# Sliding-window attention with a squared-ReLU MLP: a reordered issue plan, the last store on another queue, and the mask distances on another engine

## The chip, the cores and the metric

The kernel runs on one core of a Trainium2 chip. Five engines of that core work side by side: TensorE (PE in the profile: matrix products and transposes), VectorE (DVE), ScalarE (ACT), GpSimd (POOL) and SyncE (SP). Each takes its own instructions strictly in order, and semaphores hold an instruction back until what it needs is there. Transfers run on 16 DMA engines and are issued here from three queues: GpSimd's (loads that convert to bf16), SyncE's and ScalarE's. The metric is the device time of one execution in microseconds; lower is better. Four runs of the kernel before took between 317.31 and 318.31 us, median 317.45.

## The reference: what is computed

Attention over a window of 128 positions with a distance penalty, and a two-layer MLP on its output:

```python
# q, k, v: (8 batches, 8 heads, 576 positions, 64), float32
scores = scale * np.matmul(q, k.transpose(0, 1, 3, 2))       # scale = 1/8
rel = pos[:, None] - pos[None, :]
slopes = 2.0 ** (-8.0 * (np.arange(H) + 1) / H)
bias = slopes[:, None, None] * (-np.abs(rel))[None]
mask = (rel >= 0) & (rel < window)                             # window = 128
scores = np.where(mask, scores + bias[None], -1e9)
attn = np.exp(scores - np.max(scores, axis=-1, keepdims=True))
attn = attn / (np.sum(attn, axis=-1, keepdims=True) + 1e-09)
x = np.matmul(attn, v).transpose(0, 2, 1, 3).reshape(4608, 512)
h = x @ w_in                                                   # w_in: 512 x 2048
g = np.maximum(h, 0.0) ** 2
out = g @ w_out                                                # w_out: 2048 x 512
```

## The kernel before

**Blocks and jobs.** The 576 positions of a batch are four blocks of 128 and one of 64, 40 blocks in all. `seq` lists them in the order of work and numbers them `m` = 0 to 39: first the eight first blocks (0 to 7), then pair after pair of batches. A query block sees its own key block and the one before, so a job is a "diag" (one or two first blocks, `DIAG`), a "full" (own and previous block) or a "half" (the two 64-position blocks of a pair of batches). Attention output is collected in `xT`, transposed, in ranges of 128 columns (`ranges`); two half blocks share a range. In the kernel before, the last range is the pair of half blocks of batches 6 and 7.

**Steps of a job.** In brackets stands the name that the planner gives a step. GpSimd's queue loads K and Q (`lkq`, L387) and V (`lv`, L392). K and Q are transposed: for blocks below `N_PE` = 9 by TensorE (`tp`, L443, eight 128x128 transposes) with copies out of PSUM (`ev`); for the others by a DMA transpose from SyncE's queue (`kqT`, L429). Scores (`s`, L499), exponentials on ScalarE (`e`, L523), a multiplication by the mask on VectorE (`m`, L531 to L538), attention values (`pv`, L566: a row of ones in V gives the softmax sum), a reciprocal (`r`, L584) and a scaling (`n`, L588). The result is transposed into `xT`: below `N_PE` by TensorE (`xp`, L608) and a copy (`x`), whole or, below `N_CUT` = 4, in two parts; above it by a DMA transpose from SyncE (`x`, L596).

**The MLP.** It works in nine groups `g` of 512 tokens, four ranges each. The up-projection of group 0 is cut into pieces of 128 tokens and of groups 1 and 2 into pieces of 256 (`u`, L700); later groups take 512 at a time (`fc`, L716). A piece's result is in PSUM; ScalarE takes the ReLU into bf16 (`relu`, L671) and VectorE squares it (`sq`, L662). The down-projection `o` (L742) runs per range in four pieces of four matmuls, each needing one quarter of `w_out`; a finished range is copied out of PSUM by ScalarE or VectorE (`oe`, L271 or L273) and stored from SyncE's queue (`st`, L761). The very last range is cut into columns 0 to 383 and 384 to 511 (`CUT`), each with a copy and a store of its own. A range of two half blocks needs two stores per part.

**Buffers that tie steps together.** PSUM has eight banks: two tagged "h" (up-projection pieces, `tp`, `xp`, and the values of the first `N_PVH` = 1 jobs), two "o" (down-projection), four "a" (scores, other values). A step that takes a bank waits until the step two (or four) before it with that tag has been copied out. K and Q have a ring of four buffers in SBUF.

**What sets the order.** All steps are put as tasks into a planner (`Plan`). Each has a key, a modelled length on each engine that could do it, the tasks it depends on, and the buffers that it takes and frees. `Plan.order` lists the tasks one at a time: of each engine's candidates, those that could start within `NEAR` ns of the earliest one compete, and the lowest key wins. The instructions are then issued in exactly that order. The keys come from the order of the MLP pieces (`work_list`), with a job placed `LEAD` = 320 key units ahead of the first piece that needs it, and from `DUE` for the first jobs. The loads at the start follow `FIRST` ("b3" is block 3's K, Q and V; "i2" and "o2" are quarters of `w_in` and `w_out`). A matmul group of which the planner expects that it waits over 200 ns is preceded by padding matmuls on a constant tile (`fill`, L252), in number 0.7 of the gap.

**The start.** GpSimd makes an iota of distances (L287). VectorE derives from it the identity (L294) and, for the own-block half (`part` 1), the mask distances (L300 and L301), from which ScalarE makes the eight heads' masks (L310). The half for the previous block (`part` 0) follows later in the same way. Eight warm-up matmuls on a constant tile (L413) run on TensorE meanwhile. Block 0's K and Q come through the queues of SyncE and ScalarE, everything else through GpSimd's queue, whose loads wait each for the one eight places ahead to have landed.

Of the kernel before, what the change touches and what calls it, by code (L numbers as in the profile page):

```python
# [15 lines left out]
FIRST = ["b0", "b1", "b2", "i0", "i1", "o0", "i2", "o1", "b3", "i3", "o2", "o3", "b4", "b5", "b6", "b7"]  # L16
DIAG = [[0], [1], [2], [3], [4, 5], [6, 7]]
N_PE = 9
N_CUT = 4
N_PVH = 1  # L20
N_WARM = 8
FILL = 0.7
LEAD = 320
# [5 lines left out]
DUE = {**{m: 200.0 * m - 1e5 for m in range(40)}, **{7: -40.0}}  # L29

# [26 lines left out]
class Plan:  # L57
# [8 lines left out]
    NEAR = {"PE": 25, "ACT": 250, "DVE": 60}  # L66
# [17 lines left out]
    def order(self):  # L84
        used = {tag: [] for tag in self.bufs}
# [90 lines left out]
def kernel(  # L176
# [23 lines left out]
    for b in range(0, B, 2):  # L200
# [5 lines left out]
        ranges.append([(b, HALF), (b + 1, HALF)])  # L206
        seq += ranges[-1]
# [49 lines left out]
    def act(n):  # L257
        return n * 0.95 + 115.0
# [4 lines left out]
    def dve_p(n, rate=1):  # L263
        return n / rate / 0.96 + 185.0
# [33 lines left out]
    def build_dist(part):  # L298
        op, lim = ((ALU.is_ge, float(window)), (ALU.is_lt, 0.0))[part]
        nc.vector.tensor_scalar(far[:, part], dist[:, part], lim, 1.0e6, op0=op, op1=ALU.mult)  # L300
        nc.vector.tensor_tensor(dist[:, part], dist[:, part], far[:, part], op=ALU.add)  # L301

    t_dist, t_mask, last_mask = [None, None], [[], []], None
    for part in (1, 0):
        key = EARLY + 2 if part else -1e5 + 1100
        t_dist[part] = plan.add({"DVE": 430.0}, key, lambda part=part: build_dist(part), [t_ident], name="dist",
                                later=0.0 if part else 18000.0)
        for p in range(H):
# [3 lines left out]
            t_mask[part].append(plan.add({"ACT": act(128)}, key + 1 + p, build_mask, [t_dist[part]], name="mask"))  # L312

    def ones(ts):
        for t in ts:
            nc.vector.memset(t[:, :, D:D + 1], 1.0)
    t_ones = [plan.add({"DVE": 320.0}, EARLY + 3, lambda: ones(tiles["v0"][0:2]), name="ones"),
              plan.add({"DVE": 900.0}, -1e5 + 300, lambda: ones(tiles["v0"][2:]), name="ones", later=11000.0),
              plan.add({"DVE": 1200.0}, -1e5 + 900, lambda: ones(tiles["v"]), name="ones", later=20000.0)]
# [37 lines left out]
    def load_block(m, key):  # L357
# [35 lines left out]
        l_v = plan.add({"POOL": 890.0}, key + 0.2, fetch_v, [t_zero] if kb == HALF else [], [s_v[m]],  # L393
# [28 lines left out]
    def transpose_kq(m, due):  # L422
# [12 lines left out]
        for i in range(2):  # L435
# [14 lines left out]
            for c0, c1 in pieces:  # L450
                def evac(i=i, st=st, c0=c0, c1=c1, e=len(evs[i])):
# [4 lines left out]
                    else:  # L456
# [4 lines left out]
                                       [t_tp[i]] + evs[i], [], [st], name=f"ev{m}.{i}"))  # L461
# [191 lines left out]
    def relu_square(g, slot, last_mm, key, out_of, fused):  # L653
# [12 lines left out]
        else:  # L666
            srt = Slot("rt")

            def relu():
                srt.tile = work.tile([128, 512], BF16, tag="rt", bufs=3, name="rt")  # L670
                nc.scalar.activation(srt.tile, slot.tile, AF.Relu, bias=0.0, scale=1.0)  # L671
            tr = plan.add({"ACT": act(512)}, key, relu, [last_mm], [srt], [slot], name=f"relu{g}")
            ts = plan.add({"DVE": dve(512, 2)}, key, lambda: square(srt.tile), [tr] + g_sq[g][:1], [], [srt],
                          name=f"sq{g}")
# [128 lines left out]
```

The softmax here doesn't subtract the row's maximum and nothing guards it: scores larger than these inputs give would overflow.

## Time and profile before

| | |
|---|---|
| Median of four runs | 317.45 us |
| The profiled execution | 317.51 us |
| Its span in the profile | 315.7 us |
| TensorE busy | 305.3 us (97%), 2810 matmuls |
| VectorE and ScalarE busy | 172.8 and 173.4 us (55% each) |
| GpSimd busy | 105.6 us (33%), nearly all issue of loads |
| L742 on TensorE | 592 matmuls, 143.0 us |
| L716 and L700 on TensorE | 384 and 512 matmuls, 96.7 and 46.7 us |
| Loads and stores | 39.14 MB |

The table is read as follows. The profiled execution's own time is 1.8 us over its span: the span runs from the first to the last event that the profiler records. A busy time adds the stretches in which at least one instruction of the engine runs. Matmuls of TensorE overlap: one of 128x512 is recorded with 379 ns, but they start 216 ns apart, so the number of matmuls times their distance, not their length, tells what a change of their number is worth. A group of four such matmuls takes 0.86 us of TensorE, a piece of 16 with 128 columns 0.89, a 128x128 transpose 0.055. Names like L742 are lines of the kernel before; in the changed kernel the same code stands some 20 lines further down.

### The profile page before, as it was taken

The numbers are of one execution on the slowest core, as the hardware profiler recorded it, in microseconds if no ns is written. First come the engines' busy times: TensorE is split into PE (matmuls) and PEld (weight loads), VectorE is DVE, ScalarE is ACT, GpSimd is POOL, SyncE is SP. The second block draws the span as 40 slices with busy tenths as digits, with TensorE's granted clock in tenths as the row PEclk, the third lists the DMA queues.
The fourth block names the chain that finished last, engine by engine and source line by source line (L and its number), as shares of the span: only waits on it lengthen the run. The fifth ranks groups of instructions, "written<-read, shape, count | busy, mean of one in ns | idle before, by whom it ended". The sixth has DMA issues, their size and how long they took to land.

```text
span 315.7 us, 7140 instructions
## 1 busy us (share of the span) xinstructions
PE 305.3 (97%) x2810; PEld 175.2 (55%) x2810; DVE 172.8 (55%) x494; ACT 173.4 (55%) x340; POOL 105.6 (33%) x131
## 2 busy tenths in 40 slices
PE   6789999999999999999999999999999999999994
PEld 3677767667777655555555455545445444444442
DVE  3755567666767667676676666666663222222111
ACT  5565466668566635675655665557743444444300
POOL 8835598543623855206746007200000000000000
PEclk9999999999999999999999999999999999999999
DMA  9999999999999999949999939952211000011112
GB/s 128 189 205 190 170 195 176 153 176 143 198 160 141 169 175 174 154 91 144 168 189 166 140 95 134 199 109 70 50 52 50 35 34 33 35 33 44 57 69 66
DMA packets 164130, 39.14 MB, mean 124 GB/s; under 512 B 154752, under 2 KB 159616, under 8 KB 164096
## 3 DMA queue, kind: packets, MB, share of 16 engines
q0 software_dynamic: 114656, 18.10, 83.1%
q1 hardware_dynamic: 49152, 20.33, 33.2%
q8 instruction: 22, 0.36, 0.5%
q10 hardware_dynamic: 288, 0.26, 0.3%
q14 instruction: 12, 0.10, 0.1%
HBM read 36.70 MB, written 9.44 MB: 146 GB/s over the span
## 4 chain that ended last, share of the span: by engine, by line
PE 88%; DMA 8%; POOL 2%; issue 0%; DVE 0%; POOLq 0%
PE o L742 39%; PE h L716 27%; PE h L700 11%; PE pv L566 6%; PE s L499 5%; DMA w_out_sb<-in_moe_w_out_dram 5%; DMA w_in_sb<-in_moe_w_in_dram 3%; POOL kq L387 1%; POOL vf L392 1%; PE tp L443 1%; PE xp L608 0%; POOL w_in_sb L340 0%; POOL dist L287 0%; DVE osb L271 0%; POOLq L287 0%
## 5 line engine op out<-in xcount | busy, mean ns | idle before, releaser
L742 PE MATMUL o<-w_out_sb,g 128*128 128x512 bf16 (+2 forms) x592 | 143.0, 373 | 0.6 <-DMA w_out_sb<-in_moe_w_out_dram 0.6
L671 ACT ACTIVATE rt<-h 128x512 bf16<-128x512 f32 x144 | 85.8, 609 | 95.8 <-PE h L716 69.9
L662 DVE TENSOR_TENSOR g<-rt 128x512 bf16<-128x512 bf16 x144 | 60.1, 420 | 76.3 <-ACT rt L671 76.1
L716 PE MATMUL h<-xT,w_in_sb 128*128 128x512 bf16 x384 | 96.7, 379 | 0.0
L742 PEld LDWEIGHTS <-g 128*128 128x128 bf16 x592 | 54.0, 98 | 56.3 <-issue 0.8
L523 ACT ACTIVATE P<-s 128x512 bf16<-128x512 f32 (+1 forms) x136 | 67.0, 582 | 8.7 <-PE s L499 8.6
L716 PEld LDWEIGHTS <-w_in_sb 128*128 128x128 bf16 x384 | 35.2, 98 | 39.3
L531 DVE TENSOR_TENSOR P<-P,masks 128x512 bf16<-128x512 bf16 (+1 forms) x112 | 44.6, 405 | 15.0 <-ACT P L523 10.3
L700 PE MATMUL h<-xT,w_in_sb 128*128 128x128 bf16 (+1 forms) x512 | 46.7, 246 | 2.2 <-DMA w_in_sb<-in_moe_w_in_dram 2.2
L392 POOL DMA_DIRECT2D vt<-in_v_dram x32 | 27.0, 846 | 51.8 <-PE pv L566 48.9
L387 POOL DMA_DIRECT2D kq<-in_k_dram x39 | 33.3, 855 | 29.8 <-DMA kqT<-kq 23.5
L700 PEld LDWEIGHTS <-w_in_sb 128*128 128x128 bf16 x512 | 38.6, 98 | 6.3 <-DMA w_in_sb<-in_moe_w_in_dram 2.6
L387 POOL DMA_DIRECT2D kq<-in_q_dram x39 | 33.5, 859 | 7.2 <-PE tp L443 2.9
L588 DVE TENSOR_TENSOR x<-pv,rec 128x256 bf16<-128x256 f32 (+1 forms) x80 | 33.5, 422 | 2.6
L566 PEld LDWEIGHTS <-P 128*128 128x128 bf16 (+1 forms) x576 | 25.8, 101 | 15.5 <-DVE x L588 1.7
L584 DVE RECIPROCAL rec<-pv 128x4 f32<-128x4 f32 (+1 forms) x80 | 14.3, 179 | 20.9 <-PE pv L566 17.9
L566 PE MATMUL pv<-vt,P 128*128 128x65 bf16 (+1 forms) x448 | 24.6, 194 | 0.0
L273 ACT ACTIVATE osb<-o 128x512 f32<-128x512 f32 x23 | 13.9, 606 | 8.0 <-PE o L742 7.7
L499 PEld LDWEIGHTS <-kqT 64*128 64x128 bf16 x448 | 12.4, 94 | 7.3 <-issue 7.2
L271 DVE COPY osb<-o 128x512 f32<-128x512 f32 (+2 forms) x14 | 9.2, 654 | 12.8 <-PE o L742 12.6
L499 PE MATMUL s<-kqT 64*128 64x128 bf16 (+1 forms) x256 | 15.6, 210 | 0.0
L499 PE MATMUL s<-kqT,kqT 64*128 64x128 bf16 (+1 forms) x192 | 11.4, 210 | 0.0
(42 smaller groups left out, 100.0 us busy)
## 6 DMA issues: line engine op xcount, KB each, us to landing
out_dram<-osb SPq DMA_DIRECT2D x32, 256.0 KB, 4.2
kq<-in_k_dram POOLq DMA_DIRECT2D x31, 128.0 KB, 7.0
kq<-in_q_dram POOLq DMA_DIRECT2D x31, 128.0 KB, 7.5
vt<-in_v_dram POOLq DMA_DIRECT2D x24, 128.0 KB, 7.4
w_in_sb<-in_moe_w_in_dram POOLq DMA_DIRECT2D x4, 512.0 KB, 10.5
w_out_sb<-in_moe_w_out_dram POOLq DMA_DIRECT2D x4, 512.0 KB, 15.1
vf<-in_v_dram POOLq DMA_DIRECT2D x8, 128.0 KB, 6.6
out_dram<-osb SPq DMA_DIRECT2D x6, 128.0 KB, 2.3
```

What stands on the lines that cost most here:

```text
L387: nc.gpsimd.dma_start(view(kq[s_kq[m].idx], i), source(src, m, split))
L392: nc.gpsimd.dma_start(tile_of(s_v[m])[0:n, :, 0:D], source(v, m))
L499: nc.tensor.matmul(sS[2 * g2 + r].tile[:, jj * 256 + c0:jj * 256 + c0 + w], tile_of(s_kqT[mk])[rows, c, :], tile_of(s_kqT[mq])[rows, C + c ...
L523: nc.scalar.activation(flat(Pt[sP.idx]), sS[i].tile.rearrange("p (j t) -> p j t", j=2)[:, :, lo:hi], AF.Exp, bias=0.0, scale=scale)
L531: nc.vector.tensor_tensor(flat(Pt[sP.idx]), flat(Pt[sP.idx]), flat(masks), op=ALU.mult)
L566: nc.tensor.matmul(sv.tile[0:n, hi * (D + 1):(hi + 1) * (D + 1)], Pt[sP.idx][:, place(h)].rearrange("p t q -> p (t q)")[:, w], tile_of(s_v ...
L588: nc.vector.tensor_tensor(xt[sx.idx][0:n, hf * 256:(hf + 1) * 256].rearrange("p (h e) -> p h e", h=4), heads(sv)[0:n, :, 0:D], sr.tile[0:n ...
L662: nc.vector.tensor_tensor(o, i, i, op=ALU.mult)
L671: nc.scalar.activation(srt.tile, slot.tile, AF.Relu, bias=0.0, scale=1.0)
L700: nc.tensor.matmul(slot.tile[:, f * w:(f + 1) * w], w_in_sb[:, cc, fc * 128:(fc + 1) * 128], xT[:, cc, lo:lo + w], start=cc == 0, stop=cc ...
L716: nc.tensor.matmul(slot.tile, w_in_sb[:, cc, fc * 128:(fc + 1) * 128], xT[:, cc, g * 512:(g + 1) * 512], start=cc == 0, stop=cc == C - 1)
L742: nc.tensor.matmul(slot.tile[:, 0:hi - lo], gt[:, fc, t * 128:(t + 1) * 128], w_out_sb[:, fc, lo:hi], start=fc == 0, stop=fc == FCB - 1)
```

## The change

Four things are edited together, and the planner derives a new order from them.

1. Order: a table `ADJ` adds to the keys of 72 named tasks; `NEAR`, `LEAD`, `FIRST`, `N_PE`, `N_CUT` and `N_PVH` get other values; tasks get distinct names so that the table can name them.
2. The mask distances of part 1 (two operations on 128x128) run on GpSimd, behind the iota and ahead of the first load.
3. The pair of half blocks of batches 6 and 7 moves one range forward, so that the last range is a whole block.
4. For the last piece of output (columns 384 to 511 of the last range), the copy out of PSUM may run on ScalarE alone, and the store is issued from ScalarE's queue.

```diff
-FIRST = ["b0", "b1", "b2", "i0", "i1", "o0", "i2", "o1", "b3", "i3", "o2", "o3", "b4", "b5", "b6", "b7"]
+FIRST = ["b0", "b1", "b2", "i0", "i1", "b3", "o0", "i2", "o1", "o2", "i3", "o3", "b4", "b5", "b6", "b7"]
-N_PE = 9
-N_CUT = 4
-N_PVH = 1
+N_PE = 8
+N_CUT = 0
+N_PVH = 2
-LEAD = 320
+LEAD = 400
+ADJ = {
+    "e0.1": -99072.1, "e10.1": 230.48, "e11.2": 300.26, "e13.2": -99189.87, "e14.1": 417.51, "e14.2": 99036.91,
+    "e18.2": -99622.23, "e19.1": 40, "e2.2": 99294.7, "e3.0": 99671.0, "e3.2": 99443.6, "ev6.1.0": 99358.1,
...
+    "u2.1.6": 36.7, "u2.1.7": -239, "xp6.0": 99340.3,
+}
-    NEAR = {"PE": 25, "ACT": 250, "DVE": 60}
+    NEAR = {"PE": 60, "ACT": 25, "DVE": 0}
 def order(self):
+        for t in self.tasks:
+            t.key += ADJ.get(t.name, 0.0)
...
         jobs.append(("half", [len(seq), len(seq) + 1]))
-        ranges.append([(b, HALF), (b + 1, HALF)])
-        seq += ranges[-1]
+        seq += [(b, HALF), (b + 1, HALF)]
+        ranges.insert(len(ranges) - (b + 2 == B), seq[-2:])
...
     def build_dist(part):
         op, lim = ((ALU.is_ge, float(window)), (ALU.is_lt, 0.0))[part]
-        nc.vector.tensor_scalar(far[:, part], dist[:, part], lim, 1.0e6, op0=op, op1=ALU.mult)
-        nc.vector.tensor_tensor(dist[:, part], dist[:, part], far[:, part], op=ALU.add)
+        e = nc.gpsimd if part else nc.vector
+        e.tensor_scalar(far[:, part], dist[:, part], lim, 1.0e6, op0=op, op1=ALU.mult)
+        e.tensor_tensor(dist[:, part], dist[:, part], far[:, part], op=ALU.add)
...
-        l_v = plan.add({"POOL": 890.0}, key + 0.2, fetch_v, [t_zero] if kb == HALF else [], [s_v[m]],
+        l_v = plan.add({"POOL": 890.0}, key + 0.2, fetch_v, [t_zero] if kb == HALF else [t_dist[1]], [s_v[m]],
...
+        engs = {"ACT": act(hi - lo), "DVE": dve_p(hi - lo)}
+        if end and (g, t) == (NG - 1, 3):
+            del engs["DVE"]
+        final = end and (g, t) == (NG - 1, 3)
         def store():
             for i, (b, kb) in enumerate(ranges[4 * g + t]):
                 n = blk[kb]
-                nc.sync.dma_start(out[b * S + kb * 128:b * S + kb * 128 + n, lo:hi],
-                                  so.tile[i * 64:i * 64 + n, 0:hi - lo])
+                (nc.scalar if final else nc.sync).dma_start(
+                    out[b * S + kb * 128:b * S + kb * 128 + n, lo:hi], so.tile[i * 64:i * 64 + n, 0:hi - lo])
```

The order that results, on TensorE at the start: in the kernel before, the up-projection of block 0 follows directly on the values of block 1, and block 3's transposes come after the first pieces that need the third quarter of `w_in`. In the changed kernel the scores of block 2 and the transpose of block 1's output come ahead of the first up-projection piece, and block 3's transposes and scores come ahead of the first down-projection piece; 30 padding matmuls are issued where 54 were. On VectorE and ScalarE the number of instructions changes only by the steps named: ScalarE makes 25 output copies instead of 23, VectorE 12 instead of 14, and block 8 has no copies out of PSUM for its transposes. SyncE issues two transposing DMAs more, block 8's K and Q and its output.

## The prediction

> **What bounds the kernel now.** I read the engine totals first, then the slices of the span, then a table of TensorE's busy time by stretch, then the timeline of the stretch that is not full and of the tail.
>
> The page's totals and the slices of TensorE, then four rows of the table by stretch (busy us and instructions of PE, PEld, DVE, ACT, POOL; clock; DMA share; GB/s):
>
> ```profile
> PE 305.3 (97%) x2810; PEld 175.2 (55%) x2810; DVE 172.8 (55%) x494; ACT 173.4 (55%) x340; POOL 105.6 (33%) x131
> PE   6789999999999999999999999999999999999994
> ...
> 8.00:12.00 4.00, 3.39 (x64) 2.94 (x61) 3.71 (x19) 2.99 (x10) 4.00 (x6) 1.00 2.04 172
> 12.00:16.00 4.00, 3.02 (x55) 2.68 (x52) 2.14 (x8) 1.52 (x5) 2.82 (x4) 1.00 1.25 207
> 28.00:32.00 4.00, 3.32 (x60) 3.03 (x59) 1.85 (x7) 2.29 (x6) 2.90 (x4) 1.00 1.24 206
> 36.00:40.00 4.00, 4.00 (x62) 3.50 (x60) 1.95 (x4) 1.95 (x4) 3.97 (x5) 1.00 2.44 154
> ```
>
> TensorE is full from 36 us to its last matmul at 311.13 us: every row of the table between them shows it busy throughout. So there are only three places where time can be won: work taken off TensorE, idle or padding in the first 36 us, and the 4.6 us from the last matmul to the span's end. Over the first 36 us the rows' idle sums to 5.85 us, and the padding matmuls of L252 (54 of them, 56 ns apart) are 3.0 us more.
>
> The timeline of the start tells what TensorE waits for there; each wait ends when a weight quarter lands:
>
> ```profile
> 14.03 1.07 PE L700 MATMUL h<-xT,w_in_sb 128*128 128x128 bf16 x16 [0.93 <-DMA w_in_sb<-in_moe_w_in_dram]
> 17.24 1.06 PE L700 MATMUL h<-xT,w_in_sb 128*128 128x128 bf16 x16
> 19.73 0.59 PE L742 MATMUL o<-w_out_sb,g 128*128 128x512 bf16 x2 [0.32 <-DMA w_out_sb<-in_moe_w_out_dram]
> 22.28 3.76 PE L700 MATMUL h<-xT,w_in_sb 128*128 128x128 bf16 x64 [0.55 <-DMA w_in_sb<-in_moe_w_in_dram]
> 30.30 1.96 PE L700 MATMUL h<-xT,w_in_sb 128*128 128x128 bf16 x32 [0.68 <-DMA w_in_sb<-in_moe_w_in_dram]
> 32.81 1.02 PE L742 MATMUL o<-w_out_sb,g 128*128 128x512 bf16 x4 [0.31 <-DMA w_out_sb<-in_moe_w_out_dram]
> ```
>
> The landings follow GpSimd's order of issue. Issue time plus time to landing: first quarter of w_in 7.69 + 6.3 = 13.97, second 8.43 + 8.72 = 17.15, then w_out 19.67, w_in 22.2, w_out about 25.7, block 3's K, Q, V 25.97, 26.84, 27.7, w_in 30.27, w_out 32.77 and 35.3. A quarter of a weight takes about 2.5 us of the stream, each of a block's three loads 0.87.
>
> The tail, from the timelines of VectorE and of SyncE's queue and the list of DMA issues:
>
> ```profile
> 311.15 0.29 DVE L271 COPY osb<-o 128x128 f32<-128x128 f32 x1 [0.34 <-PE o L742]
> ...
> 312.07 0.55 SPq L761 DMA_DIRECT2D out_dram<-osb  x1
> ...
> 312.67 0.59 SPq L761 DMA_DIRECT2D out_dram<-osb  x1
> ...
> out_dram<-osb SPq DMA_DIRECT2D x2, 32.0 KB, 1.9
> ```
>
> The last 128 columns are ready at 311.44, but their two stores leave at 312.07 and 312.67, because SyncE is still issuing the two stores of the 384 columns (310.84 and 311.38). The last lands at 312.67 + 1.9 = 314.57; 1.1 us to the span's end follows.
>
> **The change part by part.**
>
> *Mask distances on GpSimd.* DVE's 0.22 us (L300) and 0.29 us (L301) leave an engine that then waited 1.87 us for the first K, so nothing is won there. The two operations go onto GpSimd between the iota and the first fetch, and all POOL loads behind them move by their length d: blocks 1 and 2 are issued every 0.87 us, and the weights follow without a gap. ScalarE's eight masks follow the distances; they ended at 5.11 us before, and its next work came at 6.84, so 1.7 us of delay are covered there. GpSimd has no row of arithmetic. Below, d is DVE's own 0.51 us; above, two of GpSimd's load issues, 2 x 0.86 = 1.7. Nearest is its iota:
>
> ```profile
> 0.84 0.34 POOL L287 IOTA dist<- 128x256 f32 x1 [0.39 <-POOLq L787]
> ```
>
> Two of these give d = 0.69, which I take. A gain is excluded, since the loads only wait longer.
>
> The Trainium skill (GPSIMD Engine Reference, section 4.1) speaks against this part: elementwise work belongs on VectorE, and GpSimd is about twice as slow with two inputs. By that rule d would be an estimated 2 x 0.51 = 1.0 us and the forecast below 0.3 us later. No row of this trace shows it.
>
> *The new start.* Block 3's loads come ahead of three quarters of w_out and the later w_in, so that TensorE has block 3 to work on while it waits. I compare one set of work: all 16 pieces of the first group's up-projection (L700, 128 tokens each), blocks 0 to 3 complete, and six pieces of L742. Before, the last of these pieces is the one at 41.12 + 0.89 = 42.01 us. By then TensorE has also done two more pieces of L742 (0.86 each) and 16 transposes for blocks 4 and 5 (0.055 each): 2.61 us. The set alone would end at 39.40.
>
> After, the first piece starts when w_in lands, 13.97 + 0.69, or about 14.7. Scores of block 2 and the transpose of block 1's output now stand ahead of that and, by the rows of the same steps, are done near 14.1. From 14.7 on: 16 pieces x 0.89 = 14.24; six of L742 x 0.865 = 5.19; four halves of attention values 0.12 each = 0.50; output transposes of blocks 2 and 3 0.45; K and Q transposes of block 3 0.45; its scores 0.35. Sum 21.2. Waits: two pieces and block 2's values end near 16.75, and the second quarter of w_in lands at 17.15 + 0.69, 1.1 us. Then twice a PSUM buffer is late: block 3's transposes follow directly on pieces whose ReLU (0.60 us, plus 0.2 before the matmul's result is there) must first free one, less a 0.22 us transpose: 0.63 each. After that the remaining quarters land ahead of their use (w_out 23.0 for 23.7, w_in 25.5 for 25.5, w_out 28.2 for 28.6, w_in 33.2 for 33.9). End: 14.7 + 21.2 + 2.4 = 38.3. Gain 1.1 us. The 24 padding matmuls fewer lie inside these waits and count nothing by themselves.
>
> Behind it the loads of blocks 4 to 7 stay d later while TensorE comes 1.1 us earlier. Before, block 7's Q landed at 38.49 + 6.9 = 45.4; 46.1 now, with its transpose due at 45.9. I charge 0.2 us (0 to 0.6).
>
> *Block 8 through the DMA (N_PE 9 to 8).* Eight transposes of L443 and four of L608 go, in a stretch where TensorE is full: 12 x 0.055 = 0.66 us gained. Two copies on VectorE (0.42 each) and one on ScalarE (0.60) go from beside it. In come a transposing DMA of K and Q and one of the output from SyncE. Block 8's Q lands near 49.4, and the first such DMA issues of before took:
>
> ```profile
> kqT<-kq SPq DMA_TRANSPOSE x1, 8.3
> ...
> kqT<-kq SPq DMA_TRANSPOSE x1, 8.8
> ```
>
> So it lands at 58.2, and the scores of block 8 come, by counting the work from 38.3, at about 59.1: hidden with 0.9 us to spare (the longest of the 31, 9.9 us, would cost 0.2). GpSimd's reload of that K and Q buffer now waits for this landing, not for a transpose at 49.9. Block 12's scores, near 82, are 24 us away; its loads, transpose and landing take some 16 of them.
>
> *Reordered pieces in groups 1 and 2, the planner's near and lead values.* No instruction is added; they decide what stands next to what. The tightest place by counting rows is near 55 us, where five pieces of the second group follow on ScalarE's four exponentials; its pitch there is 2.06 / 4 = 0.515 us against 0.87 us of a piece, and 0.1 us (0 to 0.4) may be waited once. Beyond group 2 the distances between a piece and what it needs are, by the same count, no smaller than those of before, which shows no wait. N_CUT and N_PVH change which copies and PSUM buffers the start uses; they are in its sum.
>
> *The tail.* The last range is one block of 128 rows, so each part is one store. The 384 columns leave from SyncE at 310.84 as before; the 128 columns go through ScalarE (0.3 us, as VectorE's 0.29) and its own queue, free since 300 us. Issue near 311.55, landing 1.9 to 2.2 later (the rows of 32 and 96 KB stores): 313.55 against 314.57, 1.0 us gained. With ScalarE's own rows of the start, 2.6 and 3.4 us to landing, it would be between 0.4 us gained and 0.4 lost.
>
> **Sum.** 1.1 - 0.2 + 0.66 - 0.1 + 1.0 = 2.5 us. The profiled execution took 317.51 (span 315.7 and 1.8 around it), 0.06 over the median: 315.0.
>
> **Rivals.**
> - *New waits eat the start's gain.* Loads, block 8's transpose or a ScalarE queue come later than counted. For it: margins of 0 to 0.9 us where before had 3 us (block 9's transpose landed at 59.6 for 62.65). Against: VectorE and ScalarE are 55% busy. All bounds together (d 1.7, waits 1.2 in all) leave 0.1 + 0.66 + 1.0 - 1.2: 316.9; half of that 316.0.
> - *The tail is not shortened*, if ScalarE's queue lands as late as at its start: 315.6 to 316.4. Against: those loads met an opening stream, the stores an empty one.
> - *TensorE's clock falls in the start*, as padding drops from 54 to 30. For it: the warm-up matmuls stand 0.43 us apart against 0.216 later, so there is a slow state, which the clock column does not show. Against: before idled 0.93 us at 13.1 unpadded and ran full speed after. Half speed over four pieces costs 3.6 us less the 1.1 us wait, 317.5; over two, 315.7.
> - *Slower: GpSimd's arithmetic is far slower than a row of it suggests*, through loading its program, say. All loads shift by d, so it decides from d = 0.69 + 2.5 = 3.2 us; at 6 us it is 320.4. ScalarE's table load (1.28 us) is the only loading that the trace shows. The GPSIMD Engine Reference of the Trainium skill (section 2.1, instruction dispatch) gives about 6 us for the first call of freshly loaded code; nothing here shows whether it applies.
>
> **How the numbers follow.** Forecast 0.50 (314.1 to 315.9), better than it 0.05, new waits 0.20, tail 0.07, clock 0.08, GpSimd 0.10. This kernel's measurement tells 0.3%, 0.95 us, from no change: faster is below 316.5. That takes the forecast, the better case, half of the waits, the tail and most of the clock's: 0.78. Same 0.12, slower 0.10. The range, 313.9 to 317.2, leaves out GpSimd, the worst of the clock and the best few hundredths.
>
> **What would show it.** GpSimd's two arithmetic rows sum to 0.5 to 1.0 us and the first L700 piece starts near 14.7. The table by stretch shows TensorE full from about 22 us, not 36. It stays full to the last matmul; a wait for block 7's Q, for the transpose of block 8 or near 55 us would show as idle in 44 to 60. The last matmul ends near 309.7, the last store is issued within 0.5 us of it, and the span is 313.2. A first load later than 4 us, or idle past 60 us, makes me wrong.

## The result and the profile after

The changed kernel takes 318.34 us (median of 53 runs, 315.51 to 321.63), the kernel before 317.55 (73 runs, 316.93 to 318.51): a ratio of 1.002, 95% interval 1.001 to 1.003. Medians and ranges here and below are of all runs; the ratios leave out a run that lies more than 1.5% above the fastest of its kernel. Forecast were 315.0, and a range of 313.9 to 317.2. The change is slower by a little, and far from the 2.5 us that it was to gain. The profiled execution took 319.79 us, with a span of 317.9; it is 1.45 us over the median, so the losses that it shows are those of one of the slower executions.

The engine totals and the slices of the span, of the kernel after:

```profile
PE 305.5 (96%) x2774; PEld 174.7 (55%) x2774; DVE 170.0 (53%) x490; ACT 172.5 (54%) x335; POOL 106.8 (34%) x133
...
PE   7589999999889999999999999999999999999996
...
PEclk9979999999999999999999999999999999999999
```

TensorE has 36 instructions fewer and the same busy time. Three things in these slices were not there before: a 5 for a 7 in PE's second slice (8 to 16 us), a 7 in the row of the clock, in the third slice (16 to 24 us), and two 8s in PE's row in the eleventh and twelfth slices (79 to 95 us). What TensorE waited for, from the list of waits (total, times, longest):

```profile
PE h L720 <- DMA w_in_sb<-in_moe_w_in_dram: 2.4, 1, 2.4
PE pv L586 <- DVE P L551: 1.5, 1, 1.5
PE h L720 <- DMA xT<-x: 1.2, 1, 1.2
```

Lines of the changed kernel stand 19 or 20 further down: L720 is what L700 was, L762 is L742, L449 and L616 are the transposing DMAs of K and Q and of the output (L429 and L596).

**The first loss is at the start.** GpSimd's queue, then TensorE's timeline, then four rows of the table by stretch (us in the stretch, then busy us of PE, PEld, DVE, ACT, POOL; clock; DMA share; GB/s):

```profile
1.28 0.64 POOL L320 TENSOR_SCALAR far<-dist 128x128 f32<-128x128 f32 x1
2.01 0.45 POOL L321 TENSOR_TENSOR dist<-dist,far 128x128 f32<-128x128 f32 x1
2.41 1.10 POOL L412 DMA_DIRECT2D vf<-in_v_dram  x1
```
```profile
16.57 3.49 PE L720 MATMUL h<-xT,w_in_sb 128*128 128x128 bf16 x32 [2.41 <-DMA w_in_sb<-in_moe_w_in_dram]
```
```profile
14.00:16.00 2.00, 0.16 (x3) 0.00 (x0) 0.91 (x5) 1.06 (x4) 1.33 (x2) 1.00 1.22 195
16.00:18.00 2.00, 1.43 (x15) 1.44 (x16) 0.00 (x0) 0.00 (x0) 0.75 (x1) 0.68 1.69 177
18.00:20.00 2.00, 2.00 (x23) 2.00 (x21) 0.42 (x1) 0.60 (x1) 0.00 (x0) 0.50 2.04 157
20.00:22.00 2.00, 2.00 (x41) 2.00 (x40) 1.48 (x6) 1.19 (x2) 1.39 (x2) 0.97 1.37 198
```

In the kernel before, the first load left at 1.35:

```profile
1.35 1.02 POOL L392 DMA_DIRECT2D vf<-in_v_dram  x1 [0.16 <-issue]
```

The two operations take 1.09 us on GpSimd, and the first load leaves at 2.41 rather than 1.35. The first quarter of w_in is issued at 8.91 (7.69 before) and the first piece starts at 16.57 (14.03 before). TensorE has by then waited 2.41 us, and its clock falls to half: two pieces take 3.49 us, where 1.96 is what two pieces take at full clock.

**The second loss is at 80 to 90 us**, where the table shows TensorE busy for 7.31 of 10 us. SyncE's queue there, and then three waits that follow from it, one of VectorE and two of TensorE:

```profile
59.05 18.02 SPq L449 DMA_TRANSPOSE kqT<-kq  x3
77.16 1.22 SPq L616 DMA_TRANSPOSE xT<-x  x1
78.49 3.24 SPq L449 DMA_TRANSPOSE kqT<-kq  x2
81.82 3.15 SPq L616 DMA_TRANSPOSE xT<-x  x2
```
```profile
83.87 0.42 DVE L608 TENSOR_TENSOR x<-pv,rec 128x256 bf16<-128x256 f32 x1 [2.18 <-DMA xT<-x]
...
84.69 0.20 PE L586 MATMUL pv<-vf,P 128*128 128x65 bf16 x1 [1.49 <-DVE P L551]
88.59 1.91 PE L720 MATMUL h<-xT,w_in_sb 128*128 128x256 bf16 x16 [1.20 <-DMA xT<-x]
```

The third transposing DMA of the first group (block 12's K and Q) waits for its loads until 75.84. SyncE takes its queue in order, and the transpose of block 8's output (x8), which VectorE had finished at 69.7, stands behind it and leaves at 77.16; block 9's (x9) follows at 81.82. The ring for x has three buffers, so VectorE waits 2.18 us for x8's transpose before it can write the next one, and TensorE waits behind it, and again for x9. In the kernel before, block 8's output was transposed by TensorE and is not on this queue; x9, the first output there, left at 67.97 and x10 at 75.75.

**The tail** did what it was to do, and more. The last part's copy and store, and the list of DMA issues at the end (KB each, us to landing):

```profile
314.92 0.28 ACT L292 ACTIVATE osb<-o 128x128 f32<-128x128 f32 x1 [13.26 <-PE o L762]
315.23 0.35 ACTq L786 DMA_DIRECT2D out_dram<-osb  x1
```
```profile
out_dram<-osb ACTq DMA_DIRECT2D x1, 64.0 KB, 1.6
```

From the last matmul to the span's end it is 3.0 us, 4.6 before.

**Where the time went.** Two points of TensorE's order can be found in every variant of the changed kernel: the end of the set of work that the prediction counted (16 pieces of group 0, blocks 0 to 3, six pieces of the down-projection), and the last matmul's end. The times below, of the experiments too that follow further down, are read from the timelines of TensorE; the set's end is the start of its sixth down-projection piece plus 0.89.

| kernel | first piece | set ends | last matmul ends | from set to last |
|---|---|---|---|---|
| before (set's end as the prediction worked it out) | 14.03 | 39.40 | 311.13 | 271.7 |
| forecast | 14.7 | 38.3 | 309.7 | 271.4 |
| after | 16.57 | 40.78 | 314.89 | 274.1 |
| e0_again (after, again) | 15.78 | 38.91 | 312.98 | 274.1 |
| e1_dist_dve | 16.22 | 39.31 | 313.43 | 274.1 |
| e2_pad | 16.45 | 39.99 | 311.40 | 271.4 |
| e3_swap | 16.32 | 40.41 | 311.98 | 271.6 |
| e6_all | 16.15 | 38.71 | 310.55 | 271.8 |
| e8_pad_order | 16.56 | 39.64 | 310.84 | 271.2 |
| e9_dve_order | 14.94 | 37.95 | 309.60 | 271.7 |
| e10_order | 16.94 | 41.21 | 312.41 | 271.2 |
| e11_dve_order_pad8 | 15.30 | 39.53 | 311.21 | 271.7 |
| e12_idle_pool | 16.93 | 41.12 | 312.32 | 271.2 |

The row of the kernel before holds a misreading of the prediction: its last piece of the set starts at 40.95 in the trace, not at 41.12. By the measure of the other rows its set would end at 39.23, 271.9 us ahead of the last matmul, and the forecast gain at the start would have been 0.9 us, not 1.1.

The last column has two values: 274.1 with the wait on x8, 271.2 to 271.8 without it. That wait costs about 2.6 us, and without it the rest runs as forecast. The set's end varies from 37.95 to 41.21, and that is the start. From first piece to set's end it is 23.0 to 23.5 us at full clock (e0, e1, e2, e8, e9) and 24.1 to 24.3 where the clock column shows it at half over the first pieces (after, e3, e10, e12): the fall costs 1.1 us, not the full 1.5 of the two pieces, because in full clock TensorE next waits a little, for ScalarE's ReLU (0.38 us in e0) or for the second quarter of w_in (0.34 or 0.35 in e1, e2 and e8). Two rows differ for reasons of their own: in e6 padding holds the first piece back although its weights are there (22.6 us), and in e11 TensorE waits 1.50 us for the second quarter (24.2 us at full clock).

### The profile page after: what moved, and what is told of

Read it like the earlier page. It is cut to its first block, busy times and chain, and to the rows that moved or that the text cites. A ratio compares the mean times of both kernels' runs of the same rounds, so it can differ in the third digit from the quotient of the medians.

```text
span 317.9 us, 7068 instructions
## 1 busy us (share of the span) xinstructions
PE 305.5 (96%) x2774; PEld 174.7 (55%) x2774; DVE 170.0 (53%) x490; ACT 172.5 (54%) x335; POOL 106.8 (34%) x133
## 4 chain that ended last, share of the span: by engine, by line
PE 89%; DMA 5%; POOL 2%; SPq 1%; ACT 0%; DVE 0%; issue 0%; POOLq 0%
PE o L762 37%; PE h L736 27%; PE h L720 14%; PE pv L586 6%; PE s L519 5%; DMA w_in_sb<-in_moe_w_in_dram 2%; DMA xT<-x 2%; POOL kq L407 1%; SPq L449 1%; POOL vf L412 1%; PE tp L463 1%; PE xp L628 0%; DVE x L608 0%; SPq L616 0%; POOL far L320 0%
## 5 line engine op out<-in xcount | busy, mean ns | idle before, releaser
L762 PE MATMUL o<-w_out_sb,g 128*128 128x512 bf16 (+2 forms) x592 | 142.1, 373 | 0.0
L762 PEld LDWEIGHTS <-g 128*128 128x128 bf16 x592 | 54.0, 98 | 56.1
L736 PEld LDWEIGHTS <-w_in_sb 128*128 128x128 bf16 x384 | 35.2, 98 | 39.3
L720 PE MATMUL h<-xT,w_in_sb 128*128 128x128 bf16 (+1 forms) x512 | 48.1, 251 | 4.1 <-DMA w_in_sb<-in_moe_w_in_dram 2.4
L720 PEld LDWEIGHTS <-w_in_sb 128*128 128x128 bf16 x512 | 40.1, 101 | 9.2 <-DMA w_in_sb<-in_moe_w_in_dram 2.6
L292 ACT ACTIVATE osb<-o 128x512 f32<-128x512 f32 (+1 forms) x25 | 14.7, 587 | 21.5 <-PE o L762 21.5
L586 PE MATMUL pv<-vt,P 128*128 128x65 bf16 (+1 forms) x448 | 23.6, 194 | 0.0
L290 DVE COPY osb<-o 128x512 f32<-128x512 f32 (+1 forms) x12 | 8.2, 679 | 15.0 <-PE o L762 14.9
L586 PE MATMUL pv<-vf,P 128*128 128x65 bf16 x128 | 9.7, 195 | 1.9 <-DVE P L551 1.5
```

Of the source, the lines that this page charges most:

```text
L586: nc.tensor.matmul(sv.tile[0:n, hi * (D + 1):(hi + 1) * (D + 1)], Pt[sP.idx][:, place(h)].rearrange("p t q -> p (t q)")[:, w], tile_of(s_v ...
L720: nc.tensor.matmul(slot.tile[:, f * w:(f + 1) * w], w_in_sb[:, cc, fc * 128:(fc + 1) * 128], xT[:, cc, lo:lo + w], start=cc == 0, stop=cc ...
L736: nc.tensor.matmul(slot.tile, w_in_sb[:, cc, fc * 128:(fc + 1) * 128], xT[:, cc, g * 512:(g + 1) * 512], start=cc == 0, stop=cc == C - 1)
L762: nc.tensor.matmul(slot.tile[:, 0:hi - lo], gt[:, fc, t * 128:(t + 1) * 128], w_out_sb[:, fc, lo:hi], start=fc == 0, stop=fc == FCB - 1)
```

## The experiments

### Each part of the change by itself

The whole change again, timed beside the next two kernels:

> The changed kernel as it is, profiled a second time and timed beside the next three. Theory: the fall of the clock at 16 to 20 us is there every time (granted clock near 0.6, the first two pieces of L720 over 3 us), because the first quarter of w_in lands after 16 us every time; the wait at 81 to 89 us comes and goes with where block 12's loads land, between 0 and 2.7 us, and is what spreads its runs over several us. Rival: both vary, or the spread comes from elsewhere, in which case this profile shows idle in other stretches.

Measured: 318.14 us (12 runs, 316.61 to 319.91), before 317.39 beside it, ratio 1.0016 [0.9997, 1.0036]. The theory's first half misses: the profiled execution kept the clock at 1.00 through the start after a wait of 1.95 us, with its first piece at 15.78. It had the wait on x8 (7.34 of 10 us busy from 80 to 90); whether that comes and goes, one profile cannot tell. The runs scatter over 3.3 us, those of the kernel before beside it over 1.1 (317.17 to 318.29). The clock falls in some executions and not in others, but that alone does not explain the scatter: seven of the 53 runs of the changed kernel have a mean granted clock of 1.00, which leaves no room for a fall, and they lie between 316.61 and 319.06 us.

The tail alone, in the kernel before (the last range whole, its last part through ScalarE and ScalarE's queue):

```diff
-        ranges.append([(b, HALF), (b + 1, HALF)])
-        seq += ranges[-1]
+        seq += [(b, HALF), (b + 1, HALF)]
+        ranges.insert(len(ranges) - (b + 2 == B), seq[-2:])
...
+        if end and (g, t) == (NG - 1, 3):
+            del engs["DVE"]
...
-                nc.sync.dma_start(out[...])
+                (nc.scalar if final else nc.sync).dma_start(out[...])
```

> The kernel before with the tail alone: last range a whole block, last copy on ScalarE, last store from ScalarE's queue. Theory: from the last matmul to the span's end 3.0 us as in the changed kernel, against 4.6, and nothing else moves: 1.5 us faster than before, 315.9 to 316.1, with as little spread as before. Rival: the move of the half blocks shifts the last groups' order and costs some of it: under 1 us.

Measured: 315.88 us (315.74 to 316.11), before 317.39: ratio 0.9947 [0.9936, 0.9959], 1.5 us by the medians. The tail's gain shows alone, and the time from the last matmul to the span's end is 3.0 to 3.2 us in this kernel and in every variant of the changed one. What the single store, ScalarE's queue and the new order of the last ranges each bring was not separated.

The distances of the diagonal part alone, on GpSimd in the kernel before:

```diff
-        nc.vector.tensor_scalar(far[:, part], dist[:, part], lim, 1.0e6, op0=op, op1=ALU.mult)
-        nc.vector.tensor_tensor(dist[:, part], dist[:, part], far[:, part], op=ALU.add)
+        e = nc.gpsimd if part else nc.vector
+        e.tensor_scalar(far[:, part], dist[:, part], lim, 1.0e6, op0=op, op1=ALU.mult)
+        e.tensor_tensor(dist[:, part], dist[:, part], far[:, part], op=ALU.add)
```

> The kernel before with the two mask-distance operations of part 1 on GpSimd, alone. Theory: the two rows take 1.1 us together, every load of GpSimd's queue leaves 1.1 us later, the first piece of the up-projection starts near 15.2 to 16.5 instead of 14.0, and the time rises by 0.8 to 1.5 us (more if the clock falls). Rival: block 0's Q, which shares the DMA engines with those loads, lands up to 1 us earlier, as it did in the changed kernel (cast at 5.2 us instead of 5.9), and the start of the kernel before has other waits to hide the delay in: within 0.5 us of before.

Measured: 320.53 us (319.5 to 320.91), ratio 1.009 [1.0074, 1.0106]: 3.1 us lost, twice the 1.5 that were expected at most. TensorE's timeline of this kernel shows two places, of which the expectation had only the first:

```profile
16.15 1.07 PE L701 MATMUL h<-xT,w_in_sb 128*128 128x128 bf16 x16 [1.76 <-DMA w_in_sb<-in_moe_w_in_dram]
...
49.24 0.40 PE L444 MATMUL tp<-ident,kq 128*128 128x128 bf16 x4 [0.96 <-DMA kq<-in_q_dram]
```

The first piece is 2.1 us later than before, and a later block's Q, which the kernel before never waited for, is 0.96 us late. Here the clock stayed at 1.00 until after the last matmul, so the whole of it is lateness of loads: w_in was issued 1.26 us later than before, and it landed 7.2 us after its issue rather than 6.3.

The same part taken back, in the changed kernel (both distances on VectorE):

```diff
-        e = nc.gpsimd if part else nc.vector
+        e = nc.vector
```

> The changed kernel with the two mask-distance operations of part 1 back on VectorE; every other instruction stands where it stood. Theory A (GpSimd's arithmetic holds up the loads): the first load is issued near 1.35 us instead of 2.41, the first piece of L720 starts near 14.0 to 14.8 instead of 16.57, TensorE idles under 0.6 us ahead of it, and with the shorter idle its clock stays at 1.00; the time falls by 2.5 to 4 us against the changed kernel, to about 315 to 316. Rival B (the loads are slow by themselves, or the clock falls because there is less padding, wherever the distances are): the first piece still starts after 15.5, or its first two pieces still take over 3 us, and the time falls by less than 1.5 us. The wait between 81 and 89 us stays in both.

Measured: 317.1 us (10 runs), ratio 0.9975 [0.9944, 1.0007], 1 us below the changed kernel and unclear against before. In the profiled execution the signs are those of rival B: w_in was issued at 7.57 but landed 8.6 us later, and the first piece came at 16.22. The ten runs stand in two groups, 314.6 to 316.43 (five) and 317.78 to 318.5 (five). The profiled execution, 318.27, belongs to the upper one and has the wait on x8 (7.93 of 10 us busy). So another loss was left, and it seems to come and go; that the lower group is without it is not shown, since none of it was profiled.

### The clock at the start

36 padding matmuls on the zero tile ahead of the first piece, in the changed kernel:

```diff
             fill(t_mm, bank_of(slot, "h"))
+            if (g, r, e) == (0, 0, 0):
+                for _ in range(36):
+                    nc.tensor.matmul(slot.tile[:, 0:128], warm[:, 0:128], warm[:, 0:128], start=True, stop=True)
```

> The changed kernel with 36 padding matmuls (2.0 us) put ahead of the first piece of L720, into the 2.4 us that TensorE idles there. Theory (the idle lets TensorE's clock fall, and that costs 1.5 us by itself): the granted clock stays at 1.00 between 16 and 20 us, the first two pieces take 1.8 us instead of 3.3, and the time falls by 1.0 to 1.6 us. Rival (the clock falls from the whole sparse start, or the 1.5 us are absorbed by the wait for the next weights): the clock still falls, or the pieces run fast and the time falls by less than 0.4 us.

Measured: 316.29 us (10 runs, 315.61 to 317.64), ratio 0.9968 [0.9953, 0.9983], 2 us below the changed kernel. Its timeline of TensorE, and the stretch in which the clock had fallen:

```profile
14.02 2.17 PE L719 MATMUL h<-warm 128*128 128x128 bf16 x36
16.45 1.96 PE L723 MATMUL h<-xT,w_in_sb 128*128 128x128 bf16 x32 [0.26 <-DMA w_in_sb<-in_moe_w_in_dram]
```
```profile
16.00:18.00 2.00, 1.75 (x32) 1.57 (x30) 0.00 (x0) 0.44 (x1) 0.74 (x1) 1.00 1.53 183
```

The padding takes the place of the wait, the clock stays at 1.00, and two pieces take 1.96 us. The wait on x8 is absent in this execution as well (9.91 of 10 us busy from 80 to 90), though SyncE's order is the same: x8 left at 74.50 and x9 at 80.08, 2.7 and 1.7 us earlier than in the changed kernel. So the gain of 2 us may hold some of both, and the wait on x8 is not in every execution of one and the same order. What decides it, the landing of block 12's loads or something else, was not traced further.

### The queue on SyncE

Block 12's K and Q transpose moved behind x8 in the order, nothing else:

```diff
     done = plan.order()
+    names = [t.name for t in done]
+    late = done.pop(names.index("kqT12"))
+    done.insert([t.name for t in done].index("x8") + 1, late)
```

> The changed kernel with one step moved on SyncE's queue: the transposing DMA of block 12's K and Q goes behind that of block 8's output instead of ahead of it. Theory (head of the line: block 8's output, ready at 68.4 us, is issued only at 77.2 because the step ahead of it on SyncE waits for block 12's loads, and all later outputs slip with it): block 8's output leaves near 69, TensorE's idle between 80 and 100 us falls from 2.7 us to under 0.5, and the time falls by 2 to 2.7 us. Rival (the queue or the DMA engines are simply full there): the idle only moves to the scores of block 12 or to the next output, and the time falls by less than 1 us.

Measured: 317.06 us (6 runs, 315.32 to 320.16), ratio 0.9975 [0.9946, 1.0004]. SyncE's queue in this kernel, then the table's row from 80 to 100 us of this kernel, and last the same row of the changed kernel:

```profile
69.38 1.19 SPq L616 DMA_TRANSPOSE xT<-x  x1
74.52 5.30 SPq L449 DMA_TRANSPOSE kqT<-kq  x3
79.91 3.64 SPq L616 DMA_TRANSPOSE xT<-x  x2
```
```profile
80.00:100.00 20.00, 19.89 (x230) 14.43 (x232) 13.13 (x35) 11.32 (x22) 7.49 (x9) 1.00 1.77 186
```
```profile
80.00:100.00 20.00, 17.31 (x180) 11.84 (x179) 11.08 (x32) 9.23 (x19) 7.09 (x9) 1.00 1.81 186
```

x8 leaves at 69.38 and 2.6 us of idle are gone, without any of it coming back elsewhere: the cause of the idle is shown. The time falls by less than expected, 1.1 to 1.3 us by the medians. The start is as in the changed kernel (first piece at 16.32 after a wait of 2.09, clock 0.53 from 16 to 18), the runs still scatter, and the wait that was removed is not in every execution of the changed kernel.

### The losses together

Distances on VectorE, 18 padding matmuls, block 12's transpose behind x8:

```diff
-        e = nc.gpsimd if part else nc.vector
+        e = nc.vector
...
+                for _ in range(18):
+                    nc.tensor.matmul(slot.tile[:, 0:128], warm[:, 0:128], warm[:, 0:128], start=True, stop=True)
...
+    late = done.pop(names.index("kqT12"))
+    done.insert([t.name for t in done].index("x8") + 1, late)
```

> The three together: distances on VectorE, 18 padding matmuls (1.0 us) ahead of the first piece, block 8's output ahead of block 12's K and Q on SyncE's queue. If the three causes are separate and are all that went wrong, their gains add: about 5 to 6 us less than the profiled 319.8, 314 to 315, with TensorE full from about 22 us to its last matmul, and less spread between runs. If one of them hides behind another, or a further wait follows, it stays above 316.

Measured: 316.32 us (5 runs, 314.67 to 316.48), ratio 0.9944 [0.9919, 0.997]; the profiled execution took 315.33. The gains do not add to the 314 to 315 of the expectation. The first weights had landed near 14.6 in it, and the padding held TensorE from 15.14 to 16.15: 1.0 us of it stands in the way.

Distances left on GpSimd, 36 padding matmuls, and x8 and x9 both ahead of the transposes that had blocked them:

```diff
     done = plan.order()
+    for name, behind in (("kqT12", "x8"), ("kqT13", "x9"), ("kqT14", "kqT13")):
+        late = done.pop([t.name for t in done].index(name))
+        done.insert([t.name for t in done].index(behind) + 1, late)
...
+                for _ in range(36):
+                    nc.tensor.matmul(slot.tile[:, 0:128], warm[:, 0:128], warm[:, 0:128], start=True, stop=True)
```

> The changed kernel with the 36 padding matmuls ahead of the first piece and a fuller repair of SyncE's order: outputs of blocks 8 and 9 go ahead of the K and Q transposes of blocks 12 and of 13 and 14. Theory: full clock at 16 to 20 us, no idle between 80 and 100 us, outputs of blocks 8 and 9 issued near 69 and 77 us; 315.3 to 316 with a spread under 1.5 us, ahead of the padding alone by 0.5 us. Rival: the clock alone matters; no difference from the padding alone (316.3), or the scores of block 13 wait instead.

Measured: 316.01 us (8 runs, 315.55 to 317.81), ratio 0.9959 [0.9943, 0.9976]; clock 1.00 in every run, x8 away at 68.61 and x9 at 74.47. That is 0.3 us below the padding alone, with ranges that overlap: the new order on SyncE is worth nothing clear here, and the rival (the clock alone matters) is not excluded by the times.

### The two remedies apart, and what the distances really cost

Same SyncE order as the last one, no padding, distances on VectorE:

```diff
-        e = nc.gpsimd if part else nc.vector
+        e = nc.vector
...
+    for name, behind in (("kqT12", "x8"), ("kqT13", "x9"), ("kqT14", "kqT13")):
+        late = done.pop([t.name for t in done].index(name))
+        done.insert([t.name for t in done].index(behind) + 1, late)
```

> The changed kernel with the mask distances back on VectorE and with K and Q flips 12, 13, 14 issued behind x flips 8, 9 and 9 on SyncE; no padding. Theory (two separate losses: loads on GpSimd 1.1 us later, and output x8's flip queued behind flip 12): both are gone, so the slower half of the runs that the distances alone left (317.8 to 318.5 us) disappears and what remains is its faster half, 314.6 to 316.4; median 315.0 us. Rival (the two halves come from the clock or from how the loads land, whatever the queue order): two groups again, median about 317.

The same with the distances left on GpSimd:

```diff
+    for name, behind in (("kqT12", "x8"), ("kqT13", "x9"), ("kqT14", "kqT13")):
+        late = done.pop([t.name for t in done].index(name))
+        done.insert([t.name for t in done].index(behind) + 1, late)
```

> The changed kernel with only the SyncE order changed (flip 12 behind x8, flips 13 and 14 behind x9); distances stay on GpSimd. Theory (loads 1.1 us later cost 1.5 to 2 us, as the fastest runs with and without it differ, 316.6 against 314.6): 316.5 us, 1.5 above the kernel with the distances on VectorE. Rival (the distances on GpSimd cost nothing once the mid-kernel wait is gone): 315.0, equal to it.

And with them on VectorE and the same order on SyncE, while GpSimd does the same two operations on a tile that nobody reads:

```diff
-        e = nc.gpsimd if part else nc.vector
+        e = nc.vector
+        if part:
+            nc.gpsimd.tensor_scalar(spare, dist[:, 0], lim, 1.0e6, op0=op, op1=ALU.mult)
+            nc.gpsimd.tensor_tensor(spare, dist[:, 0], spare, op=ALU.add)
...
+    for name, behind in (("kqT12", "x8"), ("kqT13", "x9"), ("kqT14", "kqT13")):
...
```

> Distances on VectorE, SyncE order as before, and GpSimd does the same two operations on a spare tile that nobody reads, ahead of its first load. The result is unchanged; GpSimd only comes to its loads 1.1 us later. Theory (the cost of the distances on GpSimd is the delay of the loads behind them): as with the distances on GpSimd, 316.5 us. Rival (it is the masks that come later, or what VectorE does in that time): as with the distances on VectorE, 315.0.

| kernel | median us | runs | ratio to before |
|---|---|---|---|
| e9, distances on VectorE | 314.77 | 5, 314.29 to 315.44 | 0.9918 [0.9904, 0.9932] |
| e12, VectorE, GpSimd busy for nothing | 317.05 | 11, 316.32 to 318.13 | 0.9990 [0.9978, 1.0001] |
| e10, distances on GpSimd | 317.5 | 12, 316.14 to 319.24 and one at 325.09 | 0.9999 [0.998, 1.0017] |

The first piece and the clock of e9 and of e10, from TensorE's timelines and the tables by stretch, e9 first:

```profile
14.94 1.95 PE L720 MATMUL h<-xT,w_in_sb 128*128 128x128 bf16 x32
```
```profile
8.00:12.00 4.00, 3.91 (x49) 3.19 (x49) 2.18 (x8) 2.50 (x8) 4.00 (x6) 0.58 2.03 174
```
```profile
16.94 3.59 PE L720 MATMUL h<-xT,w_in_sb 128*128 128x128 bf16 x32 [2.01 <-DMA w_in_sb<-in_moe_w_in_dram]
```
```profile
16.00:20.00 4.00, 3.06 (x29) 3.06 (x30) 0.59 (x2) 0.60 (x1) 0.74 (x1) 0.50 1.91 176
```

GpSimd's first load and ScalarE's masks in e12:

```profile
2.44 1.10 POOL L416 DMA_DIRECT2D vf<-in_v_dram  x1
```
```profile
3.41 1.70 ACT L334 ACTIVATE masks<-dist 128x128 bf16<-128x128 f32 x8
```

The times of e9 and e12 are within 0.6 us of what their theories had. Against e9 the distances on GpSimd cost 2.7 us and the same two operations on a spare tile cost 2.3; no run of e10 or e12 is as fast as the slowest of e9. The masks start at 3.41 us in e12 as in e9 (and at 3.36 in the changed kernel), so it is the delay of the loads, not of the masks. In the profiles it divides so: in three profiles with early loads and little or no padding (e1, e9 and, with 8 padding matmuls and no wait behind them, e11) the first piece starts at 14.94 to 16.22, on average 15.5; in the five with late ones (after, e0, e3, e10, e12) at 15.78 to 16.94, on average 16.5. That is 1.0, near the 1.3 to 1.4 us by which w_in is issued later (8.89 to 8.99 for 7.56). The fall of the clock, 1.1 us, comes in four of those five and on the first pieces of none of the three. The expectation of e10 was 1 us too low because it took the fastest of the changed kernel's runs for typical.

The padding alone separates e8 from e10, both with the new order and with the distances on GpSimd: 316.01 against 317.5, 1.5 us, near the 1.1 that the clock's fall costs in the traces (the two were timed on two chips, with medians of 317.39 and 317.43 for the kernel before).

With the distances on VectorE the new order on SyncE is worth 2.3 us (317.1 to 314.77); with them on GpSimd 0.6 (318.14 to 317.5). Neither pair was timed side by side, and the 0.6 is inside the scatter. The remedies do not add by the medians: the distances alone bring 1.0 us (e1), the order alone 0.6 (e10), both 3.4 (e9). Why is open. e9 is the best kernel of the study: 2.66 us under the kernel before.

Eight padding matmuls added to e9:

```diff
+                for _ in range(8):
+                    nc.tensor.matmul(slot.tile[:, 0:128], warm[:, 0:128], warm[:, 0:128], start=True, stop=True)
```

> Distances on VectorE, SyncE order as before, and 8 padding matmuls (0.45 us) ahead of the first piece. Theory (padding matters only where the wait for the first weights is long enough for the clock to fall, and with the loads back in their places it is 0.5 to 1 us): 315.0 us, the same as without padding within 0.5. Rival (the clock falls there all the same and 8 matmuls prevent it): 1 us below the kernel without padding, 314.0.

Measured: 315.83 us (10 runs, 313.94 to 317.66), ratio 0.9943 [0.9919, 0.9968]. No gain; the rival's 314.0 is out, and the expected 315.0 within 0.5 is missed too. In the profiled execution the second quarter of w_in landed late, and TensorE waited 1.50 us before 18.99. The scatter of 3.7 us in a kernel whose start differs from e9's by eight matmuls is not explained. It bears on the size of the cost above: e9's five runs may be lucky ones, and measured against e11 the late loads of e12 cost 1.2 us, not 2.3.

## Why the prediction was wrong, point by point

- **Mask distances on GpSimd.** The step took d = 0.69 us and named 1.7 as its upper bound. The first load came 1.06 later and w_in 1.22 later, inside the bounds, at 1.5 to 1.8 times the figure that was taken. The rival that loading a program would make it 3.2 us or more is out: the two rows are 0.64 and 0.45 us. The Trainium skill's rule (GPSIMD Engine Reference, section 4.1) was used there for an estimated 1.0 us, which was the better number, though not for its reasons: the rule has GpSimd about twice as slow with two inputs and near line rate with one, so that kept to the letter it gives an estimated 0.22 + 2 x 0.29 = 0.80. Here the two-input operation took 0.45 against VectorE's 0.29, and the one-input one 0.64 against 0.22.
- **"A gain is excluded, since the loads only wait longer"** was wrong, though it paid nothing: with GpSimd's loads later, block 0's Q, which comes through other queues, was cast at 5.19 rather than 5.92 us. But TensorE then ran out of work before the weights landed, and the head start became part of the 2.41 us wait.
- **The new start**, the first of the two steps that failed, did so twice. The first piece was put at 13.97 + 0.69 = 14.7 and came at 16.57; 0.5 us of this is d, and the rest is w_in's landing, 7.6 us after its issue where the kernel before had 6.3. Why it took longer is open: w_in landed 6.4 to 8.6 us after its issue in the profiles with early loads (e1, e6, e9, e11) and 6.8 to 8.0 in those with late ones. Then the rival "TensorE's clock falls in the start" came true, in four of the five profiles with late loads and no padding, over two pieces, as its milder version had it; and it was set aside on an argument that did not carry: that the kernel before idled 0.93 us and ran at full speed after. The wait was two and a half times as long here. "The 24 padding matmuls fewer lie inside these waits and count nothing by themselves" may be the same error: 36 padding matmuls in that wait kept the clock (e2, e8), but no run puts those 24 back. The count of the work itself held: from first piece to set's end 23.1 us in e0 and 23.0 in e9 at full clock, against 38.3 - 14.7 = 23.6 forecast.
- **Block 8 through the DMA, the planner's reordering.** From the set's end to the last matmul 271.4 were forecast, and 271.2 to 271.8 were measured wherever the wait on x8 is absent. That fits, but the spread is as large as the 0.66 us of this step, which was not measured alone.
- **The step that failed most in the profiled execution:** "Block 12's scores, near 82, are 24 us away; its loads, transpose and landing take some 16 of them." That counts block 12's own use and not what is queued behind it. Block 12 itself was in time: block 8's transposing DMA landed at 60.1 (50.74 + 9.4), block 12's own at 80.4 (75.84 + 4.6), 20 us later, for scores at 86.76. But the transpose of x8, an instruction on the same in-order queue, waited 7.4 us behind it, and a ring of three x buffers carried this to VectorE and TensorE: 2.6 us. Order on SyncE alone removes it from the trace (e3, e10); by the medians, which mix executions with and without this wait, the start is the larger loss.
- **The tail.** Forecast 1.0, measured 1.6 in the trace and 1.5 by the medians when alone. The store landed 1.6 us after its issue, not 1.9 to 2.2, and left 0.34 us after the last matmul.

Together in the profiled execution: the last matmul ends at 314.89 instead of 309.7. Of these 5.2 us the start has 40.78 - 38.3 = 2.5 and the wait on x8 2.7; the tail gives back 0.5. Without both losses the sum comes near, but by an offset: with d at 0 it would give a gain of 2.5 + 0.7 = 3.2 us for e9, which measured 2.66. Of that the tail has 1.5 instead of 1.0, so start and middle brought 1.2 where 2.2 were forecast.

## What to carry to other kernels

When an instruction on an in-order queue is made to wait longer, price what stands behind it in that queue, not the thing that it produces; a transposing DMA that waits for its load can hold up a finished output. A microsecond added ahead of the first loads is not a microsecond at the end (1.1 us cost between 1.0 and 3.1 here): look for the waits that it lengthens and for a fall of TensorE's clock in them, and count padding matmuls as cover for that, sized to the wait and no longer (36 of them separate e8 from the slower e10 by 1.5 us; 18 ahead of weights that had landed cost 1.0 in e6). And where runs of one kernel scatter by 3 us, compare points along the trace (first piece, end of a set of work, last matmul) between variants: here two columns separated three effects that the medians mixed.

## What the hardware showed that was not expected

TensorE's clock fell around waits that look alike, and not in every execution. At the end of the waits for w_in it fell in the changed kernel (2.41 us), in e3 (2.09) and in e12 (2.89), and not in e0 (1.95). In e10 it fell at 13.7 us, before the wait of 2.01, in a start that was idle in part (1.43 of 2 us busy from 12 to 14). After the waits for block 0's Q, near 7 us, it fell in e1 (2.23), e4 (1.85), e9 (2.12) and e11 (2.2), and not in e6 (1.84).

What is alike in all of them is how long it stays low. In the changed kernel's rows the clock is 0.68, 0.50 and 0.97 from 16 to 22 us: it misses 0.32, 0.50 and 0.03 of three times 2 us, which at a clock of 0.50 makes 3.4 us. The rows of e1, e3, e4, e9, e11 and e12 give 3.4 us too, and those of e10 twice that, 6.8. So one fall costs at most 1.7 us of TensorE's work. The Trainium skill (TensorE: Matmul & The Clock Gate, Part 1) has the clock halve after an idle window of about 3.4 us that runs freely and does not start with the kernel. The length agrees with that figure, and a free-running window fits that the same wait sometimes costs and sometimes not, but waits clearly shorter than the 3.4 us were enough here.

Where it falls decides what it costs. In e9 the clock was at 0.50 from 8 to 10 us, after a wait of 2.1 us for block 0's Q, and that is the fastest kernel of all: TensorE had time there, since the weights were still on their way.

The first quarter of w_in took 6.8 us from its issue to landing in e0 and 8.0 in e10, which issue it within 0.04 us of each other. Why its landing varies is open; nothing was tried on it.
